# Transposes of x and of LayerNorm's output moved to the DMA queue, and P·V with V's two parts side by side

## The chip, the cores and the metric

The kernel runs on one core of a Trainium2 chip. The metric is device time in microseconds of one execution. Shorthand for the engines: PE is TensorE (PEld its weight loads), DVE VectorE, ACT ScalarE, POOL GpSimd, SP the engine whose queue issues nearly all DMAs.

## The reference, cut to what matters

Shapes: batch 4, 8 heads, sequence 576, head dimension 64, model dimension 512. All data are float32.

```
scores = (q @ k.T) / 8                      # per batch and head, 576 x 576
scores = where(scores >= max(scores) - tau, scores, -1e9)
attn   = softmax(scores)
x      = heads of (attn @ v) side by side   # 4 x 576 x 512
xn     = (x - mean(x)) / sqrt(var(x) + 1e-6) * g
x      = x + relu(xn @ w_ch1) @ w_ch2       # 512 -> 2048 -> 512
theta  = x @ w_theta
y      = w_tok_r @ (x * cos(theta)) + w_tok_i @ (x * sin(theta))   # over the tokens
u      = x + y
out    = u + relu(u @ w_ch)
```

## The kernel before

**Precision.** Most products are made in float16 with each factor split into a high part and a low part (the remainder), and three of the four partial products are added: high·high, high·low and low·high. The exceptions are the scores (float32) and all of batch 0's attention after the scores, which stays in float32 (the batches listed in `WHOLE`).

**Tiles.** Two batches form a pair `p`: 1152 tokens, nine tiles of 128. Tiles 0 to 3 belong to the even batch, 5 to 8 to the odd one, and tile 4, the tail, holds 64 tokens of each. Tiles are grouped by three for the LayerNorm and the MLP: group `(p, gi)`.

**Attention.** `couple(b, t, hp)` handles two heads of one tile of queries. Scores go to PSUM; DVE takes the row extreme, POOL adds tau, ACT masks and exponentiates into `ringE`; then the float16 high part and the low part are written to `ringP` (high 576 columns, low 512 and 64 columns beside them), and one DMA transpose from SP's queue turns 128x1152 of it into `PT`, nine blocks of 128x128. The product P·V (`pvmm`) takes for each of five key blocks the high P against V's high part (65 columns, the last being ones, so that the sum of the row comes with it) and against V's low part (64 columns), and then four low P blocks against V's high part: 14 products per head, 28 per couple. `evict` copies 128x130 from PSUM to `x`, on ACT or DVE. A tail couple has the two heads' tails in one tile, so its weights are 64 columns wide.

**LayerNorm and the MLP.** `ln_group` normalizes three tiles, transposes each with four float32 PE transposes (L1163) into PSUM, and evicts them as a high and a low part into `ringX`, which has two places. A copy goes to DRAM for later. `mlp1` (L701) and `mlp2` (L724) then run the first 12 of 16 column chunks of the MLP during the attention (`p_A`, `chA`); the last four chunks follow after the attention for all six groups (`p_B`, `c`).

**Theta, token mixing, channel product.** When a pair's x is final, a power-of-two scale is taken from the sum of its squares (L1457, L619 to L625). `transposes(b)` turns batch b's tiles with four float32 PE transposes each (L1525), and writes high and low parts, scaled, into `x1T`; the tail tile is turned once for both batches. `thetas` (L1573), `make_z` (cosine and sine, L1647 to L1660, and the parts of z, L296 and L309), `mix` (L1737) and `chan` (L1795) follow. The order in the code is: x, theta, z of batch 0; x, theta of batch 1; mix 0, z 1, channel 0, mix 1; x, theta, z of batch 2; channel 1; x, theta of batch 3; mix 2, z 3, channel 2, mix 3, channel 3. `x1T` has two places, so batch 2's waits for the end of channel 0.

**The order of the work.** Every step is an `op` with dependencies, slots of buffers that it acquires and releases, and a cost in nanoseconds for each engine that may run it. A planner (`Plan`) plays this through, gives each step to an engine, and writes the instructions out in that order; each engine's queue runs in order, DMAs of SP included. On PE the ready step with the lowest `key` goes first: attention has low keys, the first MLP part higher ones, so that MLP blocks fill what attention leaves. After the plan the chip keeps the order and only waits on semaphores.

Of the kernel before, what the change touches and what calls it, by code (L numbers as in the profile page):

```python
# [9 lines left out]
F16 = mybir.dt.float16  # L10
# [65 lines left out]
MT = 2  # L76
IDLE = 200.0
NTINY = 960
BUSY = 0.7
LATE = 25000.0  # L80
CX = [0, 760.0, 1250.0]
CHA, CHV, CHG = [0, 680.0, 1160.0], [0, 690.0, 1290.0], [0, 758.0, 1370.0]
CLV, CLG = [0, 930.0, 1600.0], [0, 1206.0, 2060.0]
# [187 lines left out]
def tile_kernel(  # L271
# [79 lines left out]
    rY = Res("y", 0)  # L351
    rXs = Res("x", NXS)
    rN = Res("xn", 2)
    rG = Res("g", 8)
    rR = Res("raw", NRAW)
    rQ, rK = Res("q", NQ), Res("k", NK)
# [102 lines left out]
    op(warmup, [k_ones], (warm,), (warm,), T=4000, key=-1e9)  # L459


    def cvt(src, shape, hi, lo, name, start=(), acq=(), kind="cvt", peak=None, late=None, early=False):


        n = 1
        for s_ in shape:
            n *= s_
        sl = Slot(rRe if early else rR)
        st = {}

        def s0(e):
            if early:
                raw = rawe[sl.i // 2][:, sl.i % 2]
            else:
                raw = (lp if sl.i < NRAW else later["wb"]).tile([128, 512, 2], I32, tag=str(sl), name=f"raw_{name}")
            rw = st["rw"] = raw[:, 0:n, :]
            if len(shape) == 2:
                dst = rw.rearrange("p (c k) two -> p c (k two)", c=shape[0])
            else:
                dst = rw.rearrange("p k two -> p (k two)")  # L480
            Q.dma_start(dst, src)

        sa = Slot(rN)

        def s1(e):
            st["a"] = lp.tile([128, 576], F32, tag=str(sa), name=f"a_{name}")[:, 0:n]
            if e is A:
# [37 lines left out]
        def s5(e):  # L525
            if late:
                V.scalar_tensor_tensor(out=lo(), in0=st["w"], scalar=late(), in1=hi(), op0=ALU.mult, op1=ALU.subtract)
            else:
                sub(e, lo(), st["w"], f(hi()))

        kw = dict(kind=kind)
        o = load = op(s0, start, tuple(acq) + (sl,), Q=1800, **kw)
        oa = op(s1, [o], [sa], A=ac(n), V=vc(n, .7), **kw)
        ob = op(s1b, [o], A=ac(n), **kw)
        if peak:
            o = op(s2a, [oa], V=vc(n, 1.1) + 80.0, **kw)
# [12 lines left out]

        return (load, end) if late else end([])  # L550
# [182 lines left out]
    class Keys:  # L733


        def __init__(self, b, hp, prev):
# [64 lines left out]
                                scalar1=0x7F800000, scalar2=None, op0=ALU.bitwise_and)  # L801

            def one(e):
                G.memset(st["va"][:, 0].rearrange("p t (j c) -> p t j c", j=2)[:, :, :, 64:65], 1.0)

            def hi16(e):
                A.activation(out=heads(0), in_=raw(), func=AF.Copy, scale=st["sc"])
# [20 lines left out]
            o = self.sc = op(s3, [o], V=150, **kd)  # L828
            o = op(hi16, [o], A=822, **kd)
            l = op(lo16, [o], (), (sv,), V=1130, G=2200, **kd)  # L830
            o1 = op(one, [o_n], G=130, **kd)
            self.vready = [op(other, [l, o1], A=300, V=230, **kd)]

    class Queries:
# [15 lines left out]
    def couple(b, t, hp):  # L850
# [38 lines left out]
        def pvmm(w, out, j, cs):  # L889
# [4 lines left out]
                             rhs=d.st["raw"][:, t, j * 65:j * 65 + 65], start=(t == 0), stop=(t == 4))  # L894
                return
            va, pt = d.st["va"], w["pt"]
            seq = []
            for t in range(4):
                seq.append((pt[:, t, cs], va[:, 0, t], 65))
                seq.append((pt[:, t, cs], va[:, 1, t], 64))  # L900
            seq.append((pt[:, 4, cs], va[:, 0, 4], 65))
            seq.append((pt[:, 4, cs], va[:, 1, 4], 64))
            for t in range(4):
                seq.append((pt[:, 5 + t, cs], va[:, 0, t], 65))
            for k, (l, r, n) in enumerate(seq):
                T.matmul(out[:, j * 65:j * 65 + n], lhsT=l, rhs=r[:, j * 65:j * 65 + n], start=(k == 0),  # L906
                         stop=(k == len(seq) - 1))

        def pv(e):
            if "o" not in cp:  # L910
# [8 lines left out]
        def evict(e):  # L919

            pr = slice(64 * odd, 64 * odd + 64) if last else slice(0, 128)
            if tile_ not in raw:
                raw[tile_] = xs.tile([128, 520], F32, tag=str(xrl), name=f"x_{p}_{t}")
            copy(e, raw[tile_][pr, hp * 130:hp * 130 + 130], cp["o"][pr, 0:130])

        o = op(pv, pts + d.vready + [first_pv.get(tile_)], (spv,) + sx_,
               [w["spt"] for w in us] + [d.sva] + ([cp["s16"]] if whole else []), T=(PVT if whole else 950), kind="att", **kw)
        first_pv.setdefault(tile_, o)
        done = x_ops.setdefault(tile_, [])
        done.append(op(evict, [o, d.sc] + done[:1], (), (spv,), V=290, A=275, kind="evict", **kw))  # L930
        if len(done) == (8 if last else 4):
            scaled(tile_)

# [168 lines left out]
    def ln_group(p, gi, base):  # L1102
# [44 lines left out]
        for t in range(nt):  # L1147
            sn, ms = Slot(rN), Slot(rM)

            def norm(e, t=t, sn=sn):  # L1150
# [5 lines left out]
                else:  # L1156
                    V.tensor_scalar(out=st["xn", t], in0=x[p, t0 + t], scalar1=rs[:, 0, t:t + 1],
                                    scalar2=rs[:, 1, t:t + 1], op0=ALU.mult, op1=ALU.add)

            def trans(e, t=t, ms=ms):  # L1160
                st["pt", t] = m_tile(ms, [128, KB, 128], f"ptr_{nm}_{t}")
                for c in range(KB):
                    T.transpose(st["pt", t][:, c, :], st["xn", t][:, c * 128:(c + 1) * 128], ident)  # L1163
# [5 lines left out]
            def lo(e, t=t):  # L1169
                cs = slice(t * 128, (t + 1) * 128)  # L1170
                sub(V, st["xt"][:, :, 1, cs], st["pt", t], st["xt"][:, :, 0, cs])

            o = first = op(norm, [o_rs, first] + last_tr, (sn,), A=808, V=vc(512, .95), kind="ln")
            o = op(trans, [o, k_pool] + trs[-1:], (ms,) if trs else (ms, sx), (sn,), T=460, key=key - 95.0)
# [323 lines left out]
    def transposes(b):  # L1498
# [5 lines left out]

        def alloc():
            if "t" not in st:
                y = later["yp"].tile([128, KB, 2, S], F16, tag=str(sl), name=f"x1T{b}")
                st["t"] = [y[:, :, a] for a in range(2)]
            return st["t"]

        for t in range(5):
            if t == 4 and odd:
                def tail2(e):
                    for a in range(2):
                        copy(e, alloc()[a][:, :, 512:576], tails[p]["t"][:, :, a, 64:128])
                st["ops"].append(op(tail2, [tails[p]["op"]] + st["ops"][:1], (), (tails[p]["sl"],),
                                    A=2 * ac(256), V=2 * vc(256, .95)))
                continue
            ms = Slot(rM)
            ss = {}  # L1520

# [12 lines left out]

            def dst(a, t=t):
                if t < 4:
                    return alloc()[a][:, :, t * 128:(t + 1) * 128]
                if "t" not in tails[p]:
                    i = tails[p]["sl"].i
                    tails[p]["t"] = hbuf[i // 2][:, i % 2].rearrange("p a (c k) -> p c a k", c=KB)  # L1540
# [12 lines left out]
            else:  # L1553
                tails[p]["op"] = o

                def tail1(e):
                    for a in range(2):
                        copy(e, alloc()[a][:, :, 512:576], tails[p]["t"][:, :, a, 0:64])
# [363 lines left out]
```

## Time and profile before

| | |
|---|---|
| median of 3 runs | 833.95 us (833.41 to 834.34) |
| the profiled execution | 833.26 us, of which the span is 831.5 us |
| PE busy | 821.0 us, 99% of the span |
| DVE, ACT, POOL busy | 621.0, 535.0, 355.8 us |
| granted clock of TensorE | 0.999 on average |
| DMA transposes | 108, all of P |

The profile is of one execution. A row of instructions in order of time has the start, the duration, the engine, the line, the operation, output and inputs, shape, and how many such instructions are merged in it; in brackets the idle time of the engine before it and what ended that. Rows that group instructions give the count, busy time and mean of one. Line numbers are those of the kernel before.

### The profile page before, as it was taken

To read this page: it belongs to the slowest core of one execution; us is meant where nothing else is said; L and a number is where in the kernel's file an instruction comes from. 1 tells how busy PE (TensorE), PEld (TensorE's weight loads), DVE (VectorE), ACT (ScalarE), POOL (GpSimd) and SP (SyncE) were. 2 spreads that over 40 slices of the span, in tenths; PEclk is the share of its full clock that TensorE was granted. 3 is DMA by queue.
4 is the path that set the end of the run, shared out by engine and by line. 5 is a ranking of instruction groups with operands and counts; after the bars stand their busy time and mean duration, and the time that the engine had idled before them with its cause. 6 is when DMAs were issued, how large, how long until landed. Compare 5 with 4: busy or idle time off the path is not lost. (4 is left out here: it accounts for less than half of the span.)

```text
span 831.5 us, 17300 instructions
## 1 busy us (share of the span) xinstructions
PE 821.0 (99%) x6625; PEld 543.4 (65%) x6625; DVE 621.0 (75%) x1279; ACT 535.0 (64%) x987; POOL 355.8 (43%) x444
## 2 busy tenths in 40 slices
PE   9999999999999999999999999999999999999997
PEld 8888866655566576666565555555555777667776
DVE  4878799999687887787557756766577693799943
ACT  5899999999588788888535543554476351564602
POOL 1332478787285465656321212221153250465611
PEclk9999999999999999999999999999999999999999
DMA  8433699894579799697563421744033010010011
GB/s 230 143 99 122 196 207 170 187 208 97 122 132 206 137 233 184 119 165 141 131 168 94 169 94 48 249 162 177 1 97 120 27 46 13 1 44 15 16 43 58
DMA packets 173235, 101.20 MB, mean 122 GB/s; under 512 B 136289, under 2 KB 154209, under 8 KB 173153
## 3 DMA queue, kind: packets, MB, share of 16 engines
q1 hardware_dynamic: 172864, 100.10, 49.5%
q8 instruction: 52, 0.85, 0.4%
q14 instruction: 31, 0.25, 0.1%
q10 hardware_dynamic: 288, 0.00, 0.0%
HBM read 52.50 MB, written 15.73 MB: 82 GB/s over the span
## 5 line engine op out<-in xcount | busy, mean ns | idle before, releaser
L701 PEld LDWEIGHTS <-w 128*128 128x128 f16 x1152 | 110.5, 98 | 80.7 <-issue 7.3
L701 PE MATMUL p_A<-ringX,w 128*128 128x384 f16 x864 | 149.9, 326 | 0.0
L724 PE MATMUL chA<-w,hbuf 128*128 128x512 f16 x648 | 149.2, 379 | 0.0
L724 PEld LDWEIGHTS <-hbuf 128*128 128x128 f16 x864 | 82.5, 99 | 93.6 <-issue 5.4
L979 DVE TENSOR_SCALAR_CACHE_REDUCE ringE<-S,ncoef 128x576 f32<-128x576 f32 x144 | 112.7, 812 | 27.2 <-PE S L878 21.1
L309 POOL TENSOR_TENSOR ringP<-ringE,ringP 128x512 f16<-128x512 f32 (+2 forms) x110 | 109.2, 1004 | 21.0 <-ACT ringP L296 16.1
L995 ACT ACTIVATE ringE<-ringE,tiny 128x576 f32<-128x576 f32 x144 | 105.5, 770 | 2.0 <-POOL tiny L987 1.0
L878 PE MATMUL S<-kf,qf 64*128 64x288 f32 (+1 forms) x576 | 98.5, 426 | 0.0
L1737 PE MATMUL y<-tok,z 128*128 128x288 f16 x768 | 97.2, 286 | 0.0
L1737 PEld LDWEIGHTS <-z 128*128 128x128 f16 x768 | 75.1, 98 | 19.2
L1021 ACT ACTIVATE ringE<-ringE,ntaup 128x576 f32<-128x576 f32 x108 | 78.6, 764 | 0.1
L707 ACT ACTIVATE hbuf<-p_A 128x384 f16<-128x384 f32 x72 | 35.2, 488 | 63.1 <-PE p_A L701 62.6
L878 PEld LDWEIGHTS S<-kf,qf 64*128 64x128 f32 (+1 forms) x576 | 56.9, 186 | 19.5 <-issue 4.5
L906 PEld LDWEIGHTS <-PT 128*128 128x128 f16 (+1 forms) x1680 | 57.3, 100 | 12.8 <-issue 5.4
L300 POOL TENSOR_SCALAR ringP<-ringE 128x576 f16<-128x576 f32 x63 | 44.7, 712 | 36.8 <-ACT ringE L1021 30.4
L906 PE MATMUL pv<-va,PT 128*128 128x65 f16 (+3 forms) x1680 | 60.2, 193 | 0.0
L1213 DVE SCALAR_TENSOR_TENSOR x<-chA,qs,x 128x512 f32<-128x512 f32 x54 | 40.3, 747 | 25.5 <-PE chA L724 25.3
L710 DVE SCALAR_TENSOR_TENSOR hbuf<-p_A,hbuf 128x384 f16<-128x384 f32 x72 | 39.6, 551 | 22.7 <-ACT hbuf L707 22.2
L724 PE MATMUL c<-w,hbuf 128*128 128x512 f16 x216 | 51.0, 379 | 0.0
L701 PE MATMUL p_B<-ringX,w 128*128 128x384 f16 x288 | 50.7, 326 | 0.0
L1795 PE MATMUL o<-x1T,cw 128*128 128x288 f16 x384 | 48.0, 286 | 1.3 <-DVE x1T L1770 1.3
L309 DVE TENSOR_TENSOR ringP<-ringE,ringP 128x512 f16<-128x512 f32 (+2 forms) x58 | 44.0, 768 | 2.9 <-ACT ringP L296 1.4
(228 smaller groups left out, 1392.8 us busy)
## 6 DMA issues: line engine op xcount, KB each, us to landing
raw_w<-in_w SPq DMA_DIRECT2D x20, 512.0 KB, 4.5
rawe<-in_w SPq DMA_DIRECT2D x12, 512.0 KB, 4.8
raw_tok<-in_wtok SPq DMA_DIRECT2D x12, 432.0 KB, 4.4
qf<-in_qT SPq DMA_DIRECT2D x20, 256.0 KB, 3.5
kf<-in_kT SPq DMA_DIRECT2D x16, 288.0 KB, 4.0
xscr<-x SPq DMA_DIRECT2D x18, 256.0 KB, 2.4
xl<-xscr SPq DMA_DIRECT2D x18, 256.0 KB, 5.1
out<-uo SPq DMA_DIRECT2D x16, 288.0 KB, 2.1
```

The costliest lines, as they stand in the source:

```text
L300: G.tensor_scalar(out=out, in0=in_, scalar1=1.0, scalar2=0.0, op0=ALU.mult, op1=ALU.add)
L309: e.tensor_tensor(out=out, in0=a, in1=b, op=ALU.subtract)
L701: T.matmul(st["ps"][:, :n], lhsT=ch.w1(a, c), rhs=xt()[:, c, bb, :n], start=(kk == 0), stop=(kk == 11))
L724: T.matmul(ps, lhsT=h[:, a, t * 128:(t + 1) * 128], rhs=ch.w2(bb), start=(first and (a, bb) == M2[0]), stop=(stop and (a, bb) == M2[2]))
L878: T.matmul(w["S"][:, n, 0:288], lhsT=qd.q["f"][r, hp], rhs=d.k["f"][r, n * 288:(n + 1) * 288], start=True, stop=True)
L906: T.matmul(out[:, j * 65:j * 65 + n], lhsT=l, rhs=r[:, j * 65:j * 65 + n], start=(k == 0), stop=(k == len(seq) - 1))
L979: V.tensor_scalar(out=st["e"].rearrange("p (a k) -> p a k", a=2), in0=st["S"][:, :, 0:288], scalar1=ncoef, scalar2=None, op0=ALU.mult, op1 ...
L995: A.activation(out=st["e"], in_=st["e"], func=AF.Prelu, bias=cp["thr"][:, j:j + 1], scale=-1.0, alpha=STEEP)
L1021: A.activation(out=e_of(ws), in_=e_of(ws), func=AF.Exp, bias=ntaup, scale=1.0)
L1213: V.scalar_tensor_tensor(out=x[p, t0 + t], in0=st["ch", t], scalar=chunks[i].quad.inv, in1=x[p, t0 + t], op0=ALU.mult, op1=ALU.add)
L1737: T.matmul(st["ps"][n][:, 0:288], lhsT=a, rhs=w[:, n * 288:(n + 1) * 288], start=(k == 0 and q == 0), stop=(k == 8 and q == 2))
L1795: T.matmul(st["ps"][n][:, 0:288], lhsT=w[:, cs], rhs=d["t"][a][:, kk, n * 288:(n + 1) * 288], start=(kk == 0 and q == 0), stop=(kk == 3 an ...
```

## The change

- `XQ = (0, 1, 2)`: for batches 0, 1 and 2 `transposes(b)` writes the scaled high and low part of each x tile, in its own orientation, into a buffer of float16 (one of the slots for raw weights), high and low blocks of 128 columns in turn, and one DMA transpose of 128x1024 on SP's queue turns it into `x1T`. Batch 3 goes by PE as before.
- `LNQ = ((1, 0), (1, 1))`: for these two groups `ln_group` does the same with the normalized tiles, into `ringX`.
- `PVW = (2, 3)`: for these two batches V's low part gets a 65th column of zeros, and P's high block is multiplied with V's high and low part in one product of 130 columns; the low P blocks go into the high part's columns. The two parts are added when they leave PSUM: `evict` becomes a reduction over two on DVE.

```diff
+NX16 = 2
+LNQ = ((1, 0), (1, 1))
+PVW = (2, 3)
+XQ = (0, 1, 2)
...
+    rX16 = Res("x16", NX16)
...
             def one(e):
-                G.memset(st["va"][:, 0].rearrange("p t (j c) -> p t j c", j=2)[:, :, :, 64:65], 1.0)
+                for a in range(2 if b in PVW else 1):
+                    G.memset(st["va"][:, a].rearrange("p t (j c) -> p t j c", j=2)[:, :, :, 64:65], 1.0 - a)
...
+            for t in range(9):
+                n = 130 if t < 5 else 65
+                T.matmul(out[:, j * 130:j * 130 + n], lhsT=pt[:, t, cs], rhs=va[:, :, t, js] if t < 5 else va[:, 0, t - 5, js],
+                         start=(t == 0), stop=(t == 8))
...
-            copy(e, raw[tile_][pr, hp * 130:hp * 130 + 130], cp["o"][pr, 0:130])
+            to = raw[tile_][pr, hp * 130:hp * 130 + 130]
+            if whole or b not in PVW:
+                copy(e, to, cp["o"][pr, 0:130])
+            else:
+                o2 = cp["o"][pr, 0:260].rearrange("p (j a c) -> p j a c", j=2, a=2)
+                V.tensor_reduce(out=to.rearrange("p (j c) -> p j c", j=2), in_=o2.rearrange("p j a c -> p j c a"), op=ALU.add,
+                                axis=mybir.AxisListType.X)
...
+            if (p, gi) in LNQ:
+                o = first = op(norm, [o_rs, first], (sn,), A=808, V=vc(512, .95), kind="ln")
+                o = op(hi_t, [o], (s16,), A=ac(512), V=vc(512, .95), G=CHG[1] - 60.0, kind="lnev")
+                o = op(lo_t, [o], (), (sn,), V=vc(512, V2), G=gc(512), kind="lnev")
+                o = op(turn_t, [o] + xt[:1], () if xt else (sx,), (s16,), Q=1800, kind="lnev")
+                xt.append(o)
+                continue
...
+            def hi_t(e, parts=parts, xin=xin):
+                scopy(e, parts()[:, :, 0, :], xin(), px(p, X_S))
+            def lo_t(e, parts=parts, xin=xin):
+                V.scalar_tensor_tensor(out=parts()[:, :, 1, :], in0=xin(), scalar=px(p, X_S), in1=parts()[:, :, 0, :], op0=ALU.mult,
+                                       op1=ALU.subtract)
+            def turn_t(e, parts=parts, turned_=turned_):
+                Q.dma_start_transpose(out=turned_(), in_=parts().rearrange("p c a k -> p (c a k)"))
...
+            if b in XQ:
...
+                o = op(hi_t, [xf[p, t0 + t], sx_ops[p], st.get("hi")], acq, A=ac(512), V=vc(512, .95), G=CHG[1] - 60.0, kind="ev")
+                st["hi"] = o
+                o = op(lo_t, [o], (), (x_slot[p, t0 + t],), V=vc(512, V2), kind="ev")
+                o = op(turn_t, [o] + st["ops"][:1], (), (s16,), Q=1800, kind="ev")
```

## Rows read from the trace of the kernel before

**Rows 1.** Page, part 1: busy us (share of the span) and instructions.

```profile
PE 821.0 (99%) x6625; PEld 543.4 (65%) x6625; DVE 621.0 (75%) x1279; ACT 535.0 (64%) x987; POOL 355.8 (43%) x444
```

**Rows 2.** Busy time by stretch: length, engines, clock, DMA share, GB/s.

```profile
232.00:300.00 68.00, 68.00 (x694) 43.18 (x691) 56.94 (x124) 56.41 (x98) 41.78 (x58) 1.00 0.88 170
300.00:340.00 40.00, 40.00 (x407) 25.89 (x406) 29.10 (x71) 33.81 (x63) 22.34 (x37) 1.00 0.95 181
...
683.00:708.00 25.00, 25.00 (x206) 20.07 (x205) 9.56 (x17) 2.33 (x3) 0.00 (x0) 1.00 0.12 48
708.00:760.00 52.00, 50.36 (x330) 32.31 (x329) 44.91 (x62) 31.28 (x51) 29.95 (x27) 1.00 0.06 24
```

**Rows 3.** Waits of PE: us in total, times, longest.

```profile
PE pt L1525 <- DVE r_t L1591: 1.6, 1, 1.6
```

**Rows 4.** Groups of PE by line and shape: count, busy, mean.

```profile
L1163 PE MATMUL ptr<-ident,xn 128*128 128x128 f32 x72 | 10.8, 278 | 0.0
...
L1525 PE MATMUL pt<-ident,xl 128*128 128x128 f32 x72 | 9.4, 274 | 1.6 <-DVE r_t L1591 1.6
```

**Rows 5.** PE in order of time, transposes of batch 2's x.

```profile
707.58 1.91 PE L1525 MATMUL pt<-ident,xl 128*128 128x128 f32 x16
709.32 1.63 PE L1795 MATMUL o<-x1T,cw 128*128 128x288 f16 x12
```

**Rows 6.** Line 1042, P's DMA transposes: ns min/median/max; us to landing.

```profile
L1042 SPq DMA_TRANSPOSE PT<-ringP x108: 1242/1337/2912, 99.6 to 422.7; - x108
...
DMA to landing us min/median/max: 3.2/3.6/6.7
```

**Rows 7.** DVE in order of time, the last step of x's scale.

```profile
589.44 0.15 DVE L625 TENSOR_SCALAR cs<-cs 128x1 int32<-128x1 int32 x1 [0.66 <-POOL cs L622]
```

**Rows 8.** PE in order of time, batch 0's theta and first mixing's tail.

```profile
594.51 10.52 PE L1573 MATMUL th<-th,x1T 128*128 128x512 f16 x48
...
648.78 0.90 PE L1737 MATMUL y<-tok,hbuf 128*128 128x288 f16 x6
```

**Rows 9.** SP's queue in order of time, P's transposes.

```profile
309.02 8.56 SPq L1042 DMA_TRANSPOSE PT<-ringP  x4
...
381.28 24.54 SPq L1042 DMA_TRANSPOSE PT<-ringP  x10
```

**Rows 10.** PE in order of time, LN's transposes and P·V around 310.

```profile
303.97 0.60 PE L1163 MATMUL ptr<-ident,xn 128*128 128x128 f32 x4
304.40 1.01 PE L906 MATMUL pv<-va,PT 128*128 128x65 f16 x28
305.25 0.63 PE L1163 MATMUL ptr<-ident,xn 128*128 128x128 f32 x4
...
306.69 0.60 PE L1163 MATMUL ptr<-ident,xn 128*128 128x128 f32 x4
...
312.27 1.07 PE L906 MATMUL pv<-va,PT 128*64 128x65 f16 x28
313.28 1.47 PE L724 MATMUL chA<-w,hbuf 128*128 128x512 f16 x6
...
323.39 1.14 PE L701 MATMUL p_A<-ringX,w 128*128 128x384 f16 x6
```

**Rows 11.** Groups of DVE by line and shape: the copy of P·V.

```profile
L298 DVE COPY x<-pv 128x130 f32<-128x130 f32 x18 | 5.2, 286 | 4.3 <-PE pv L906 2.7 <-PE pv L893 1.3
```

**Rows 12.** POOL in order of time, last part of z's tail.

```profile
639.49 1.15 POOL L309 TENSOR_TENSOR hbuf<-r_t,hbuf 128x512 f16<-128x512 f32 x1 [1.02 <-ACT hbuf L296]
```

**Rows 13.** DVE in order of time, last part of group (1,2).

```profile
447.43 0.68 DVE L309 TENSOR_TENSOR ringX<-ptr,ringX 128x512 f16<-128x512 f32 x1
```

**Rows 14.** PE in order of time, the end of attention.

```profile
420.30 2.69 PE L906 MATMUL pv<-va,PT 128*128 128x65 f16 x84
...
455.29 5.04 PE L701 MATMUL p_A<-ringX,w 128*128 128x384 f16 x30
```

More of the change, by code (lines that the diff above doesn't have):

```diff
@@ L459, in tile_kernel, with raw_tile @@
     op(warmup, [k_ones], (warm,), (warm,), T=4000, key=-1e9)
+    def raw_tile(slot, name):
+        return (lp if slot.i < NRAW else later["wb"]).tile([128, 512, 2], I32, tag=str(slot), name=name)
     def cvt(src, shape, hi, lo, name, start=(), acq=(), kind="cvt", peak=None, late=None, early=False):
@@ L474, in s0 @@
             else:
-                raw = (lp if sl.i < NRAW else later["wb"]).tile([128, 512, 2], I32, tag=str(sl), name=f"raw_{name}")
+                raw = raw_tile(sl, f"raw_{name}")
             rw = st["rw"] = raw[:, 0:n, :]
@@ L830, in __init__ @@
             l = op(lo16, [o], (), (sv,), V=1130, G=2200, **kd)
-            o1 = op(one, [o_n], G=130, **kd)
+            o1 = op(one, [o_n], G=260 if b in PVW else 130, **kd)
             self.vready = [op(other, [l, o1], A=300, V=230, **kd)]
@@ L896, in pvmm @@
             va, pt = d.st["va"], w["pt"]
[L897 to L907, printed above, removed]
+            js = slice(j * 65, j * 65 + 65)
+            if b not in PVW:
+                seq = [(t, va[:, a, t], 65 - a) for t in range(5) for a in range(2)] + [(5 + t, va[:, 0, t], 65) for t in range(4)]
+                for k, (t, r, n) in enumerate(seq):
+                    T.matmul(out[:, j * 65:j * 65 + n], lhsT=pt[:, t, cs], rhs=r[:, j * 65:j * 65 + n], start=(k == 0),
+                             stop=(k == len(seq) - 1))
+                return
+            for t in range(9):
+                n = 130 if t < 5 else 65
+                T.matmul(out[:, j * 130:j * 130 + n], lhsT=pt[:, t, cs], rhs=va[:, :, t, js] if t < 5 else va[:, 0, t - 5, js],
+                         start=(t == 0), stop=(t == 8))
         def pv(e):
@@ L923, in evict @@
                 raw[tile_] = xs.tile([128, 520], F32, tag=str(xrl), name=f"x_{p}_{t}")
-            copy(e, raw[tile_][pr, hp * 130:hp * 130 + 130], cp["o"][pr, 0:130])
+            to = raw[tile_][pr, hp * 130:hp * 130 + 130]
[5 more added lines that the diff above has]
+                                axis=mybir.AxisListType.X)
         o = op(pv, pts + d.vready + [first_pv.get(tile_)], (spv,) + sx_,
-               [w["spt"] for w in us] + [d.sva] + ([cp["s16"]] if whole else []), T=(PVT if whole else 950), kind="att", **kw)
+               [w["spt"] for w in us] + [d.sva] + ([cp["s16"]] if whole else []), T=(PVT if whole else 850 if b in PVW else 950), kind="att", **kw)
         first_pv.setdefault(tile_, o)
         done = x_ops.setdefault(tile_, [])
-        done.append(op(evict, [o, d.sc] + done[:1], (), (spv,), V=290, A=275, kind="evict", **kw))
+        done.append(op(evict, [o, d.sc] + done[:1], (), (spv,), kind="evict", **(dict(V=290, A=275) if whole or b not in PVW else dict(V=430)), **kw))
         if len(done) == (8 if last else 4):
@@ L1158, in norm, with parts, hi_t, lo_t @@
                                     scalar2=rs[:, 1, t:t + 1], op0=ALU.mult, op1=ALU.add)
+            s16 = Slot(rX16)
+            def parts(t=t, s16=s16):
+                if ("x16", t) not in st:
+                    st["x16", t] = ap.tile([128, KB, 2, 128], F16, tag=str(s16), name=f"xn16_{nm}_{t}")
+                return st["x16", t]
+            def hi_t(e, t=t, parts=parts):
+                copy(e, parts()[:, :, 0, :], st["xn", t].rearrange("p (c k) -> p c k", c=KB))
+            def lo_t(e, t=t, parts=parts):
+                sub(e, parts()[:, :, 1, :], st["xn", t].rearrange("p (c k) -> p c k", c=KB), parts()[:, :, 0, :])
+            def turn_t(e, t=t, parts=parts):
+                st["xt"] = ringX[:, sx.i]
+                Q.dma_start_transpose(out=st["xt"][:, :, :, t * 128:(t + 1) * 128].rearrange("p c a k -> p (c a) k"),
+                                      in_=parts().rearrange("p c a k -> p (c a k)"))
             def trans(e, t=t, ms=ms):
@@ L1506, in alloc @@
             if "t" not in st:
-                y = later["yp"].tile([128, KB, 2, S], F16, tag=str(sl), name=f"x1T{b}")
-                st["t"] = [y[:, :, a] for a in range(2)]
-            return st["t"]
+                st["y"] = later["yp"].tile([128, KB, 2, S], F16, tag=str(sl), name=f"x1T{b}")
+                st["t"] = [st["y"][:, :, a] for a in range(2)]
+            return st["y"]
         for t in range(5):
@@ L1514, in tail2, with parts @@
                     for a in range(2):
-                        copy(e, alloc()[a][:, :, 512:576], tails[p]["t"][:, :, a, 64:128])
+                        copy(e, alloc()[:, :, a, 512:576], tails[p]["t"][:, :, a, 64:128])
                 st["ops"].append(op(tail2, [tails[p]["op"]] + st["ops"][:1], (), (tails[p]["sl"],),
                                     A=2 * ac(256), V=2 * vc(256, .95)))
+                continue
+            s16 = Slot(rR)
+            ss = {}
+            def parts(ss=ss, s16=s16, t=t):
+                if "t" not in ss:
+                    ss["t"] = raw_tile(s16, f"x16_{b}_{t}").bitcast(F16).rearrange("p k two -> p (k two)")[:, 0:1024].rearrange(
+                            "p (c a k) -> p c a k", c=KB, a=2)
+                return ss["t"]
@@ new lines, in xin, with turned_ @@
+            def xin(t=t):
+                return x[p, t0 + t].rearrange("p (c k) -> p c k", c=KB)
+            def hi_t(e, parts=parts, xin=xin):
[3 more added lines that the diff above has]
+                                       op1=ALU.subtract)
+            def turned_(t=t):
+                if t < 4:
+                    return alloc()[:, :, :, t * 128:(t + 1) * 128].rearrange("p c a k -> p (c a) k")
+                i = tails[p]["sl"].i
+                tails[p]["t"] = hbuf[i // 2][:, i % 2].rearrange("p a n -> p (a n)").rearrange("p (c a k) -> p c a k", c=KB, a=2)
+                return tails[p]["t"].rearrange("p c a k -> p (c a) k")
@@ new lines, in turn_t, with tail1 @@
+            def turn_t(e, parts=parts, turned_=turned_):
+                Q.dma_start_transpose(out=turned_(), in_=parts().rearrange("p c a k -> p (c a k)"))
+            if b in XQ:
+                acq = [s16]
+                if t == 0:
+                    acq.append(sl)
+                if t == 4:
+                    tails[p] = {"sl": Slot(rG, 3)}
+                    acq.append(tails[p]["sl"])
+                o = op(hi_t, [xf[p, t0 + t], sx_ops[p], st.get("hi")], acq, A=ac(512), V=vc(512, .95), G=CHG[1] - 60.0, kind="ev")
+                st["hi"] = o
+                o = op(lo_t, [o], (), (x_slot[p, t0 + t],), V=vc(512, V2), kind="ev")
+                o = op(turn_t, [o] + st["ops"][:1], (), (s16,), Q=1800, kind="ev")
+                if t < 4:
+                    st["ops"].append(o)
+                else:
+                    tails[p]["op"] = o
+                    def tail1(e):
+                        for a in range(2):
+                            copy(e, alloc()[:, :, a, 512:576], tails[p]["t"][:, :, a, 0:64])
+                    st["ops"].append(op(tail1, [o] + st["ops"][:1], (), (tails[p]["sl"],), A=2 * ac(256), V=2 * vc(256, .95)))
@@ L1536, in dst @@
                 if t < 4:
-                    return alloc()[a][:, :, t * 128:(t + 1) * 128]
+                    return alloc()[:, :, a, t * 128:(t + 1) * 128]
                 if "t" not in tails[p]:
@@ L1557, in tail1 @@
                     for a in range(2):
-                        copy(e, alloc()[a][:, :, 512:576], tails[p]["t"][:, :, a, 0:64])
+                        copy(e, alloc()[:, :, a, 512:576], tails[p]["t"][:, :, a, 0:64])
                 st["ops"].append(op(tail1, [o] + st["ops"][:1], (), (tails[p]["sl"],), A=2 * ac(256), V=2 * vc(256, .95)))
```

## The prediction

> **What bounds the kernel now.** I read the page's busy times first, then busy time by stretch, then what TensorE waited for, and last its instructions in order of time around each edit. TensorE (PE) is busy 821.0 of 831.5 us, the next engine, VectorE (DVE), 621.0 [rows 1]. That a pipelined PE looks busy proves little, so the stretches count: from 232 to 340 us (attention of batches 2 and 3 mixed with the first MLP) and from 683 to 708 (token mixing of batch 1) PE has no gap at all, at a granted clock of 1.00, its 2.4 GHz level, while DVE sits at 73 to 84% in the attention and at 9.56 of 25 us in the mixing [rows 2]. Only from 708 to 760 does PE lose 1.64 us, nearly all of it in one wait of 1.6 us of an x transpose for DVE [rows 2, 3]. So PE's own instruction stream sets the end, and an edit is worth the PE time from its first instruction to the start of what follows. The rows' busy column is no price: a burst's last matmul overlaps the next burst. I take start to start.
>
> **The transposes of x.** Batch 0 has five tiles, batch 1 four (its tail is shared) and batch 2 five: 14 tiles of four float32 transposes, 56 of the 72 of that line [rows 4]. Sixteen of them, the largest of batch 2's bursts, run from 707.58 to 709.32, where the next matmul starts: 0.109 us each [rows 5]. 56 x 0.109 = 6.1 us leave PE.
>
> What comes instead: per tile a scaled float16 copy, a subtraction (both were there already, reading PSUM; now they read SBUF) and one DMA transpose of 128x1024 on SP's queue. The trace has 108 DMA transposes of 128x1152: 1.34 us of queue each, landing after 3.2 to 6.7, median 3.6 us [rows 6]. Is the longer way hidden?
>
> Batch 2: its copies need the buffer that batch 0's channel product frees, which stands ahead of batch 1's mixing in the order of the code; its theta product comes only after that mixing, at 708. From 683 to 708 DVE, ScalarE and POOL are nearly idle and DMA stands at 0.12 [rows 2]; five tiles of about 1.4 us of copies and 2.1 us of transfer fit into 25 us. It also takes the copies out of the crowded stretch 708:760 (DVE 44.91 of 52 us). Batch 1: its x is final before batch 0's theta products, and blocks of the second MLP part follow those, likewise hidden. Batch 0 is the delicate one. The scale of x is ready at 589.6 [rows 7]; copy and subtraction take about 1.4 us, a transpose 3.6 us to land, so the first tile is there at about 594.6, where the first theta matmul stood at 594.51 [rows 8]. Four transposes in a row occupy SP for 8.56 us, 2.1 us each, in a crowded stretch [rows 9]; a theta tile is 12 products of 512 columns, 12 x 0.213 = 2.6 us at 2.4 GHz, so the later tiles arrive faster than PE consumes them, and until then PE has blocks of the MLP's second part. Cost: 0 to 0.5 us, taken as 0. If that cover were gone, each us of late landing would be a us.
>
> The Trainium skill, DMA: Bandwidth & Descriptors, section "Latency and other measured facts", says that a DMA transpose with a non-contiguous middle dimension runs at 261 GB/s against 350 to 400 contiguous, a hit of some 30%. That speaks against this edit, because the new destinations are strided rows of x's buffer where P's were whole. By it a turn in a crowd would take 2.1 x 1.3 x 8/9, an estimate of 2.4 us, still under a theta tile, and the sum would stay.
>
> **LN's two groups.** Groups (1,0) and (1,1), three tiles each: 24 of the 72 transposes of that line [rows 4]. One tile takes 0.43 us (303.97 to 304.40) [rows 10]: 6 x 0.43 = 2.6 us off PE. Six DMA transposes are added where DMA is busy 0.88 to 0.95 [rows 2]. The last tile of (1,0) is turned at 306.69, its group's first product starts at 323.39, 16 us later [rows 10]; so a landing of even 6.7 us is covered, and the P transposes that queue behind a turn are 2 us late each time, while PE runs MLP blocks. Cost taken: 0; without the cover it is those 2 us for each of six turns.
>
> **PV in one product.** A full couple of heads issues 28 products of 64 or 65 columns; it will issue 10 of 130 and 8 of 65 (columns: 1810 before, 1820 after). 28 take 0.85 us (304.40 to 305.25) [rows 10], 30.4 ns each, of which 65 columns at 2.4 GHz are 27.1 and 3.3 are fixed. A product of 130 has no row: with the same fixed part 57.5 ns; at best bare columns, 54.2; at worst twice a 65, 60.8. New couple: 10 x 57.5 + 8 x 30.4 = 818 against 851 ns. I take the 0.033, the ends being 0 and 0.066, because the fixed part is the nearest row's own. 32 couples: 1.0 us (0 to 2.1). The 8 tail couples load weights of 64 columns and are slower, 1.01 us for 28 (312.27 to 313.28) [rows 10], 36.1 ns each. If the load sets that, a product of 130 hides it, and 10 x 57.5 + 8 x 36.1 saves 0.146 us; if it is a fixed part of 9 ns an instruction, 0.09; at worst nothing. I take 0.12, so 1.0 us (0 to 1.2). Together 2.0 us (0 to 3.3).
>
> On those tail couples, the Trainium skill, TensorEngine Tiling (Array Packing), section "Restrictions", says that column tiling disables fast weight load. The trace agrees so far as the 64-column bursts are the slower ones; by the rule the saving there is the upper figure, 1.2 us, and the sum 10.9.
>
> Against it stands the eviction: a copy of 128x130 from PSUM, on ScalarE or DVE, becomes a DVE reduction over 260 elements, 40 times. DVE's copy took 0.286 us [rows 11]; the reduction lies between that and twice it, 0.57; I take 0.45, nearer the upper end, because it reads twice the elements. DVE gains 40 x 0.45 = 18 us less the copies it loses (half of the 18, 3 us), 15 us over some 200; in the attention of rows 2 its 86 of 108 us (80%) would be about 87%: beside PE as long as PE has MLP blocks to run. If that cover went, 40 x 0.17 = 7 us would come out.
>
> **The sum.** 6.1 + 2.6 + 2.0 = 10.7 us. The profiled execution took 833.26 us, 1.76 around its span, which stay; it lies 0.69 under the median. 833.26 - 10.7 = 822.6, at the level of the median **823.3**. The 1.64 us of gaps in 708:760 I leave where they are.
>
> **Rivals.** (1) The attention edits buy nothing, because DMA and the elementwise engines, not PE, pace that stretch, and PE only runs MLP blocks earlier and idles later. For it: DMA at 0.95, and 15 more us on DVE. Against it: no gap in PE from 232 to 340. It would keep the x part alone, 833.95 - 6.1 = about 828.
>
> (2) Theta and z of batch 0 become the wait. The last of z's parts for the first mixing is written at 640.6 [rows 12] and read at 648.78 [rows 8], 8.1 us later. Batches 0 and 1 take 36 x 0.109 = 3.9 us of PE out of the path between, so 4.2 us of slack are left. Should the landings be at the slowest of rows 6 (issue 2.9, landing 6.7), the fifth theta tile would start some 7 us late, 3 us would be lost, and twice that if the second batch suffers as well: 826 to 829.
>
> (3) Slower: the matmuls that cover the end of attention run out. Group (1,2), the last, needs the last attention tile. Its parts are done at 448.1 [rows 13]; its first product starts at 455.29, when (1,1)'s matmuls are through [rows 14]: 7.2 us of slack. The attention had another 14 us between a long row of P transposes, issued by 405.8 [rows 9], and the PV behind it at 420.30 [rows 14]. Should each of the six turns hold up the queue by 5 us, between the median landing and the slowest, 30 us, and the reductions add 7, the 37 us would overrun the 21 us of slack by 16 and more than eat the sum: 833.95 - 10.7 + 16 = 839; at a delay of 34 us it is 836. It decides from 21 us of delay on, and from 32 us the kernel is slower than before. Against it: transfers overlap, a queue slot is 2 us and not 5.
>
> (4) The whole order is planned anew, so waits of 1 to 3 us can open anywhere, or the present ones close. With the gap at 740 gone and PV at its upper end: 833.95 - 6.1 - 2.8 - 3.3 - 1.6 = 820; with 6 us of new waits 829.
>
> (5) It cancels out, within 0.2%, where (1) and (2) come together with such waits.
>
> **How the numbers follow.** Forecast with the good half of (4), 817 to 827: 0.66. (1) 0.10; (2) with the bad half of (4) 0.09; (5) 0.05; (3) 0.10. The forecast's own range is 819 to 827; the range for 8 times in 10 runs from 817 to 831. Faster by over 0.2% (under 832.3; about what can be told from no change): 0.85; within: 0.05; slower: 0.10.
>
> **What would show it.** Right: 16 PE transposes left of the x line and 48 of LN's; 128 DMA transposes; 1280 PV products, a couple in about 0.82 us; PE still without gaps from 232 to 440 and around 590 to 610; theta of batch 2 directly behind the mixing of batch 1; PE's busy time near 810. Wrong: PE waiting at the first theta matmul for a DMA, at the first product of (1,2) for LN, or at PV for the reduction; a product of 130 columns at 61 ns; a granted clock below 1.00 in a stretch before the last. A gap of over 10 us in PE anywhere would overturn the forecast.

## The result, and the profile after

The changed kernel takes **821.38 us** (median of 4 runs, 820.92 to 822.14); the kernel before took 833.68 (4 runs, 833.28 to 834.34). The ratio is 0.9853, with a 95% interval of 0.9836 to 0.9870: 12.3 us faster. The forecast was 823.3 us, or 10.7 us off the profiled execution. The profiled execution after took 821.73 us with a span of 819.9, so 11.6 us less span than before.

First the page of the changed kernel, the row that answers to [rows 1]: busy us (share of the span) and instructions.

```profile
PE 811.4 (99%) x6145; PEld 533.8 (65%) x6145; DVE 622.7 (76%) x1291; ACT 531.7 (65%) x966; POOL 371.2 (45%) x462
```

PE has 480 instructions less: 56 + 24 transposes, and 40 couples with 10 products fewer each. Its busy time fell by 9.6 us, to the forecast "near 810", and the span by 2 us more than that. So besides PE work, idle time of PE is gone. DVE's busy time rose by 1.7 us only and POOL's by 15.4 (against [rows 1]). The waits show which (engine, line, tile, what it waited for: us in total, times, longest). After:

```profile
PE pvs L798 <- ACT va L791: 1.0, 1, 1.0
PE warm L454 <- POOL ones L420: 1.0, 1, 1.0
PE pw_w L607 <- ACT tiny L601: 1.0, 1, 1.0
PE pt L1617 <- DVE r_t L1683: 0.2, 1, 0.2
```

Before, the same list had one more row beside that of [rows 3]:

```profile
PE o L1795 <- DVE x1T L1770: 1.3, 1, 1.3
```

The first three waits after are as before. Of the 1.6 us of [rows 3] 0.2 is left, and the 1.3 us at batch 2's channel product is gone.

Busy time by stretch after (length, PE, PEld, DVE, ACT, POOL, clock, DMA share, GB/s); the first three rows answer to the last three of [rows 2], shifted by the time saved ahead of them:

```profile
292.00:332.00 40.00, 40.00 (x345) 27.03 (x344) 33.04 (x77) 32.63 (x58) 29.18 (x43) 1.00 0.95 186
...
674.00:700.70 26.70, 26.70 (x220) 21.32 (x219) 16.33 (x25) 6.35 (x11) 3.81 (x3) 1.00 0.46 95
700.70:752.00 51.30, 51.08 (x337) 32.87 (x336) 43.09 (x59) 30.83 (x51) 27.93 (x26) 1.00 0.06 24
700.00:790.00 90.00, 89.78 (x653) 63.80 (x651) 71.07 (x94) 47.92 (x80) 45.61 (x39) 1.00 0.07 27
```

In the attention PE still has no gap. In the mixing of batch 1 (second row) DVE does 16.33 us where it did 9.56, and DMA stands at 0.46 instead of 0.12: that is batch 2's x, turned under the mixing. Behind it PE idles for 0.22 us of 90. In the kernel before, the 90 us from 700 on read so:

```profile
700.00:790.00 90.00, 87.04 (x629) 61.57 (x627) 75.40 (x97) 49.53 (x82) 48.58 (x40) 1.00 0.05 17
```

That is 2.96 us idle. Now PE in order of time after (start, duration, engine, line, operation, tiles, shape, count), for [rows 5, 8, 10]:

```profile
0.98 7.31 PE L454 MATMUL warm<-ones 128*128 128x128 f32 x40 [0.98 <-POOL ones L420]
...
305.87 0.98 PE L915 MATMUL pv<-va,PT 128*128 128x130 f16 x18
306.68 0.81 PE L732 MATMUL chA<-w,hbuf 128*128 128x512 f16 x3
...
316.53 1.01 PE L915 MATMUL pv<-va,PT 128*64 128x130 f16 x18
317.48 1.24 PE L887 MATMUL S<-kf,qf 64*128 64x288 f32 x8
...
583.60 2.06 PE L1498 MATMUL px<-cs,ones 128*128 128x1 f32 x18
...
595.26 2.75 PE L1665 MATMUL th<-th,x1T 128*128 128x512 f16 x12
597.85 2.10 PE L732 MATMUL c<-w,hbuf 128*128 128x512 f16 x9
599.79 7.93 PE L1665 MATMUL th<-th,x1T 128*128 128x512 f16 x36
...
636.05 4.21 PE L1829 MATMUL y<-tok,z 128*128 128x288 f16 x33
...
700.73 10.52 PE L1665 MATMUL th<-th,x1T 128*128 128x512 f16 x48
...
713.68 11.92 PE L1887 MATMUL o<-x1T,cw 128*128 128x288 f16 x96
725.44 2.37 PE L1829 MATMUL y<-tok,z 128*128 128x288 f16 x18
...
802.67 11.93 PE L1887 MATMUL o<-x1T,cw 128*128 128x288 f16 x96
```

And the same milestones in the kernel before:

```profile
0.97 6.16 PE L449 MATMUL warm<-ones 128*128 128x128 f32 x40 [0.97 <-POOL ones L415]
...
586.51 2.06 PE L1457 MATMUL px<-cs,ones 128*128 128x1 f32 x18
...
642.90 2.37 PE L1737 MATMUL y<-tok,z 128*128 128x288 f16 x18
...
711.23 10.52 PE L1573 MATMUL th<-th,x1T 128*128 128x512 f16 x48
...
734.47 1.63 PE L1737 MATMUL y<-tok,z 128*128 128x288 f16 x12
...
814.98 11.92 PE L1795 MATMUL o<-x1T,cw 128*128 128x288 f16 x96
```

This gives the account. Up to the sum for x's scale (`px`) the lead is 2.9 us; the 40 matmuls that warm TensorE up at the start, which the change doesn't touch, took 1.15 us longer in this profile, so the attention is worth 4.1. At the first mixing it is 6.85: another 3.95, which is 36 transposes of 0.109 us. At the mixing of batch 2 it is 9.03: another 2.2, the 20 transposes of batch 2. At the last channel product it is 12.3 (814.98 against 802.67): another 3.3, of which 2.7 is idle time of PE that is gone, all of it behind 725. 4.1 + 3.95 + 2.2 + 3.3 is 13.5; less the 1.15 at the start that is the 12.3. From that product's start to the end of the span this profile takes 17.2 us and the one before 16.5, a difference of 0.7 that no edit explains; so 11.6 of the 12.3 are left in the span. The medians, which no single start or end decides, differ by 12.3.

The new DMA transposes on SP's queue after, x's (L1587, the two into `hbuf` are the tail tiles) and LN's (L1190) beside P's (L1057); count, ns min/median/max, first and last start, then us from issue to landing:

```profile
L1587 SPq DMA_TRANSPOSE x1T<-x x12: 1231/1288/2145, 589.7 to 685.5; - x12
L1587 SPq DMA_TRANSPOSE hbuf<-x x2: 1232/1272/1311, 597.4 to 686.9; - x2
...
DMA to landing us min/median/max: 3.0/3.3/5.0
...
L1190 SPq DMA_TRANSPOSE ringX<-xn x6: 1232/1351/1631, 316.3 to 397.0; - x6
...
DMA to landing us min/median/max: 3.3/4.1/5.1
...
L1057 SPq DMA_TRANSPOSE PT<-ringP x108: 1242/1345/3082, 100.8 to 419.9; - x108
...
DMA to landing us min/median/max: 3.2/3.7/7.2
```

With the 108 of P that makes the 128 that the prediction named. x's turns land a little sooner than P's, and LN's six, in the busiest stretch, a little later. P's own are about where [rows 6] had them. Five of x's in a row on the queue:

```profile
589.67 7.44 SPq L1587 DMA_TRANSPOSE x1T<-x  x5
```

### The profile page after: what moved, and what is told of

Read it like the earlier page. It is cut to its first block, busy times and chain, and to the rows that moved or that the text cites. A ratio compares the mean times of both kernels' runs of the same rounds, so it can differ in the third digit from the quotient of the medians.

```text
span 819.9 us, 16404 instructions
## 1 busy us (share of the span) xinstructions
PE 811.4 (99%) x6145; PEld 533.8 (65%) x6145; DVE 622.7 (76%) x1291; ACT 531.7 (65%) x966; POOL 371.2 (45%) x462
## 4 chain that ended last, share of the span: by engine, by line
PE 95%; ACT 2%; DVE 1%; issue 1%; POOL 0%; DVEq 0%; ACTq 0%; POOLq 0%
PE chA L732 17%; PE p_A L709 17%; PE y L1829 13%; PE S L887 11%; PE p_B L709 6%; PE c L732 6%; PE th L1665 5%; PE pv L902 5%; PE o L1887 4%; PE pv L915 4%; PE tm L965 2%; PE pv L910 2%; PE warm L454 1%; PE th_t L1665 1%; PE ptr L1196 1%
## 5 line engine op out<-in xcount | busy, mean ns | idle before, releaser
L304 POOL TENSOR_SCALAR ringP<-ringE 128x576 f16<-128x576 f32 x59 | 42.6, 725 | 37.0 <-ACT ringE L1036 34.3
L1887 PEld LDWEIGHTS <-cw 128*128 128x128 f16 x384 | 37.6, 98 | 9.7
L308 ACT ACTIVATE x1T<-u,cs 128x576 f16<-128x576 f32 x16 | 12.3, 770 | 47.7 <-DVE u L1856 41.9
```

The costliest lines, as they stand in the source:

```text
L304: G.tensor_scalar(out=out, in0=in_, scalar1=1.0, scalar2=0.0, op0=ALU.mult, op1=ALU.add)
L1887: T.matmul(st["ps"][n][:, 0:288], lhsT=w[:, cs], rhs=d["t"][a][:, kk, n * 288:(n + 1) * 288], start=(kk == 0 and q == 0), stop=(kk == 3 an ...
```

## The experiments

In the expectations A is the account that I held when the run was sent (each edit is worth the PE time that it removes; from the two traces, the closed gaps come from batch 2's x), and B is the rival named there. Differences are against the median of the kernel before on the same chip; where the changed kernel itself is the measure, its ratio 0.9853 is compared.

**x alone.** LN and P·V as before.

```diff
-LNQ = ((1, 0), (1, 1))
-PVW = (2, 3)
+LNQ = ()
+PVW = ()
```

> Only the x transposes of batches 0 to 2 go by DMA; LN's stay on PE and P.V is as before. Theory A (each edit is worth the PE time it takes away, and batch 2's x also closes the gaps of PE between 708 and 790 us): 56 x 0.109 = 6.1 us plus about 2.9 us of gaps, 833.7 - 9.0 = 824.7 us, PE without a gap over 0.5 us after 700. Theory B (the closed gaps come from LN's and P.V's edits, or from the new order as a whole): 833.7 - 6.1 = 827.6 us, with the wait of about 1.6 us for DVE at batch 3's transposes still there.

825.84 against 833.67 us, ratio 0.9903 (0.9888 to 0.9918): 7.8 us off, between the two. PE behind 700 is as full as in the changed kernel (89.77 of 90 us), so the closed gaps belong to x. About 1 us of what is missing is lost in the attention, where no edit acts, only the new order: x's scale (`px`) starts at 588.47 against 586.51, of which 0.95 us is a longer warm-up at the start. PE has these waits that neither kernel had:

```profile
PE pv L910 <- DVE tiny L589: 0.9, 1, 0.9
PE pv L910 <- ACT x L300: 0.5, 1, 0.5
```

In return the wait of 1.0 us for `va` is down to 0.3. From 0 to 240 us PE is busy 236.5 us, 237.1 before; so only 0.6 of the 1 us is idle time.

**P·V alone, LN alone, and batch 2's x alone.**

```diff
 # P.V alone
+LNQ = ()
+XQ = ()
 # LN alone
+PVW = ()
+XQ = ()
 # batch 2's x alone
+LNQ = ()
+PVW = ()
+XQ = (2,)
```

> Only the product of 130 columns for batches 2 and 3, with the reduction at eviction; all transposes on PE. Theory A (PE sets the end of the attention stretch): 32 couples x 0.031 + 8 tail couples x 0.06 = 1.5 us off, 832.2 us. Theory B (the attention stretch is paced by DVE and DMA, to which the reductions add 14 us): no gain or a loss, 833.7 us or more.

832.92 us, ratio 0.9988 (0.9979 to 0.9997): 0.75 us off, with an interval of 0.25 to 1.75 us. The gain is there and small; A's 1.5 lies inside, "nothing" doesn't. In the trace `px` starts at 585.43 against 586.51, behind a warm-up longer by 0.26 us: 1.3 us.

> Only LN of groups (1,0) and (1,1) turned by DMA. Theory A (PE sets the end): 24 x 0.109 = 2.6 us off, 831.1 us. Theory B (DMA, busy 0.9 in this stretch, paces it, and six more turns take the place of what PE saves): 833.7 us or more, with waits of PE at P.V or at the first MLP product.

831.13 us, ratio 0.9971 (0.9960 to 0.9982): 2.5 us off (1.5 to 3.3), as 6 x 0.43 says. In this kernel and in the one with P·V alone the waits of 1.6 and 1.3 us stand unchanged.

> Only the x of batch 2 goes by DMA. Theory A (its 20 transposes leave PE, and its copies leave the crowded stretch behind 708 us, which closes the gaps of PE there): 2.2 + 2.9 = 5.1 us off, 828.6 us. Theory B (the gaps close for another reason): 2.2 us off, 831.5 us, with the wait of about 1.6 us for DVE still there.

828.31 us, ratio 0.9935 (0.9922 to 0.9947): 5.4 us off. The 20 transposes are worth 2.2; here, without any other edit, the wait of 1.6 us is down to 0.2 and that of 1.3 is gone. Of the edits, batch 2's x is the one that closes the gaps.

**The transposes of batches 0 and 1 alone.**

```diff
+LNQ = ()
+PVW = ()
+XQ = (0, 1)
```

> Only the x of batches 0 and 1 goes by DMA. Theory A (PE's own time counts and the landings are hidden): 36 x 0.109 = 3.9 us off, 829.8 us, the two waits of PE behind 708 us still there (about 2.9 us). Theory B (batch 0's theta waits for its landings, or z is late for the first mixing): less than 2 us off, 831.7 us or more, with a wait of PE at theta or at the mixing.

830.89 against 833.92 us, ratio 0.9969 (0.9958 to 0.9981): 3.0 us off where the PE time says 3.9. PE waits nowhere at theta or the first mixing; the waits of 1.6 and 1.3 us are as in the kernel before, and before 240 us the new order has opened ones of 0.9, 0.5 and 0.2 us and closed the one of 1.0 for `va` (PE busy 236.4 us from 0 to 240, 237.1 before).

**Do the gaps close by the order alone, with no PE time saved?** The kernel before, with batch 2's transposes still on PE, but put by their key to the head of batch 1's mixing.

```diff
-        key = nkey() if b else KEY0
+        key = (nkey() - (1.5 if b == 2 else 0.0)) if b else KEY0
```

> The kernel before with one edit: PE's transposes of batch 2's x, and so their copies, stand ahead of batch 1's token mixing instead of behind it. PE has exactly the work of before. Theory A (the gaps behind 708 us close because batch 2's x is ready when the mixing ends, so theta starts earlier and the elementwise work behind it too): about 2.7 us off without any PE time saved, 831.0 us. Theory B (they close only because transposes leave PE): no change, 833.7 us, with the waits of 1.6 and 1.3 us still there.

831.81 us, ratio 0.9976 (0.9966 to 0.9986): 2.1 us off (1.2 to 2.8) without a single PE instruction less. Of PE's waits the two old ones are gone but for 0.2 us, and one of 0.9 is new (line numbers of the kernel before):

```profile
PE pt L1525 <- DVE x1T L1547: 0.9, 1, 0.9
PE pt L1525 <- DVE r_t L1591: 0.2, 1, 0.2
```

And in order of time its stretch behind the mixing:

```profile
710.89 0.90 PE L1737 MATMUL y<-tok,hbuf 128*128 128x288 f16 x6
711.62 10.52 PE L1573 MATMUL th<-th,x1T 128*128 128x512 f16 x48
...
724.58 11.92 PE L1795 MATMUL o<-x1T,cw 128*128 128x288 f16 x96
```

Theta follows the mixing at once and all 96 products of channel 1 stand behind it, as in the changed kernel. In the kernel before twelve of the 96 had to cover the copies of x [rows 5], and 84 were left for the longer wait; that this is why PE waited is argued, not shown. The price is the 0.9 us where the early transposes wait for their own evictions. This run moves the copies of x out of the stretch as well: DVE is busy 70.32 of the 90 us from 700 on, 75.40 before. So it shows that the place of batch 2's transposes and copies closes the gaps, and not which of the two does it, theta's early start or the lighter DVE.

**Is it the work taken off DVE?** The changed kernel with five dead DVE operations, as long as the subtractions (0.69 us each), that theta has to wait for; four of the five run behind batch 1's mixing, the first under it.

```diff
+                if b == 2:
+                    def late(e, t=t):
+                        ...
+                        V.scalar_tensor_tensor(out=later["dead"], in0=later["dead"], scalar=1.0, in1=later["dead"], op0=ALU.mult,
+                                               op1=ALU.subtract)
+                    o = op(late, [o, ylast[0]], V=690, kind="ev")
```

> The changed kernel with five idle DVE operations of about 0.75 us each (one per tile of batch 2, on a buffer of their own, result unused) placed behind batch 1's token mixing and ahead of batch 2's theta, where the subtractions of batch 2's x stood in the kernel before; nothing else is added, and PE's work is that of the changed kernel. Theory A (the gaps of PE between 708 and 790 us closed because DVE work left that stretch): most of the 2.9 us of gaps come back, 823 to 824.5 us. Theory B (they closed because of the order of PE's own instructions there, transposes ahead of theta): nothing comes back, 821.4 to 822 us.

822.06 against 834.29 us, ratio 0.9858 (0.9841 to 0.9874): as the changed kernel. One wait of 1.2 us opens (PE's mixing for POOL's `z`; PE busy 88.75 of the 90 us from 700 on), but the two old ones don't come back. DVE's busy time there is 73.29 us, so half of the 4.3 us that had gone is back; and 12 channel products stand ahead of theta again, with 30 more inside it. The old waits stay away all the same. So this run bears out neither account alone, that of the lighter DVE or that of the twelve products.

**More of the same: batch 3's x, LN's five groups, three groups, P·V of three batches.**

```diff
 # batch 3 as well
+XQ = (0, 1, 2, 3)
 # LN, five groups
+LNQ = ((0, 0), (0, 1), (0, 2), (1, 0), (1, 1))
 # LN, three groups
+LNQ = ((0, 2), (1, 0), (1, 1))
 # P.V, three batches
+PVW = (1, 2, 3)
```

> Batch 3's x goes by DMA as well, the other edits as in the changed kernel. Theory A (PE's own time counts): 16 x 0.109 = 1.7 us off, 819.7 us. Theory B (its buffer comes free only when batch 1's channel product ends, so copies of 1.4 us and a landing of 3.3 us stand ahead of its first theta product, in the stretch where DVE is at 84%): the gaps come back, 821.4 us or more.

825.07 us, ratio 0.9889 (0.9874 to 0.9903): 3.0 us slower than the changed kernel. PE in order of time at batch 3's theta:

```profile
734.16 12.15 PE L1665 MATMUL th<-th,x1T 128*128 128x512 f16 x48 [3.86 <-DMA x1T<-x]
746.14 1.63 PE L1829 MATMUL y<-tok,z 128*128 128x288 f16 x12
```

Here PE has no work ready to cover the turns: batch 3's landings are waited for, 3.9 us, and the 48 products then take 12.15 us instead of 10.52. The granted clock is 0.90 from 730 to 735, 0.75 from 735 to 740 and 1.00 from 740 on:

```profile
730.00:735.00 5.00, 1.14 (x6) 0.30 (x4) 5.00 (x7) 3.54 (x7) 2.77 (x2) 0.90 0.85 210
735.00:745.00 10.00, 10.00 (x42) 4.32 (x41) 8.08 (x12) 4.09 (x6) 6.13 (x5) 0.88 0.41 91
```

> LN by DMA in five groups, the three of the first pair added. Theory A (PE's own time counts wherever PE has no gap): nine tiles x 0.435 = 3.9 us off, 817.5 us. Theory B (from 100 to 200 us DMA is busy 0.85 to 1.07 and DVE 98%, so nine more turns there make P's transposes late and PE waits): 821.4 us or more, with waits of PE at P.V or at the MLP's first product before 240 us.

827.50 us, ratio 0.9917 (0.9903 to 0.9932): 5.3 us slower than the changed kernel, where nine tiles less on PE promised 3.9 us of gain. Busy time in steps of 5 us:

```profile
160.00:165.00 5.00, 2.47 (x34) 1.83 (x34) 5.00 (x9) 5.00 (x10) 5.00 (x6) 0.81 0.49 111
165.00:170.00 5.00, 4.19 (x31) 3.08 (x32) 5.00 (x9) 4.51 (x8) 4.12 (x4) 0.50 0.73 141
170.00:175.00 5.00, 5.00 (x40) 3.22 (x37) 5.00 (x13) 3.31 (x7) 3.96 (x6) 0.66 1.33 177
175.00:180.00 5.00, 4.97 (x51) 2.95 (x47) 4.68 (x13) 4.16 (x8) 3.70 (x6) 1.00 1.10 217
```

Around 160 us nothing but attention is ready for PE, and DVE (5.00 of 5), ACT and POOL set the pace; PE loses 3.3 us in three waits and then runs at the 1.2 GHz level (0.50) for a while. Here the cover that the prediction counted on, MLP blocks, isn't there: from 157 to 178 us PE has only attention and matmuls that fill time (`warm`).

> The changed kernel with LN of group (0,2) by DMA too, near 245 us, where DVE is below 90%. Theory A (a group outside the stretch where DVE is saturated gives back its PE time): 12 x 0.109 = 1.3 us off, 820.1 us. Theory B (its first product stands about 10 us behind its transposes, and a copy from SBUF plus a landing of 4 us under load use that up): 821.4 us or more, with a wait of PE before 260 us.

823.44 against 833.92 us, ratio 0.9876 (0.9863 to 0.9890): A's further gain fails here too, with some 2 us more than the changed kernel, though the two intervals overlap at their ends. Between 254 and 261 us PE has no MLP block, and the plan fills with 17 `warm` matmuls, 2 us together:

```profile
257.01 1.16 PE L462 MATMUL warm<-one 128*128 128x256 bf16 x9
...
260.12 1.05 PE L462 MATMUL warm<-one 128*128 128x256 bf16 x8
```

That is not the whole of it: a wait of 0.7 us for V's parts (`va`) opens at 254.5, and before 240 us PE has the waits of the run with x alone again (0.8 and 0.5 us, 0.5 us less busy from 0 to 240), at a place that this group doesn't touch.

> The product of 130 columns in batch 1 as well. Theory A (PE's own time counts): 16 couples x 0.031 + 4 x 0.06 = 0.7 us off, 820.7 us. Theory B (20 reductions of 0.42 us more on DVE, which is at 98% from 120 to 200 us, have no cover): about 20 x 0.42 = 8 us more on DVE less the copies it did, part of it on the path: 823 to 828 us.

822.61 us, ratio 0.9866 (0.9851 to 0.9881): with 0.8 us of PE time on offer (16 couples of 0.033 and 4 tails of 0.06 us) it is not faster than the changed kernel, and if anything 1 us slower, which the intervals don't decide. PE has new waits of 0.9, 0.7 and 0.3 us and loses an old one of 1.0; from 100 to 590 us it is busy 1.0 us less than in the changed kernel, more than the edit had to give.

**Does the reduction cost anything?** The eviction copies the high part alone and leaves V's low part out.

```diff
-                V.tensor_reduce(out=to.rearrange("p (j c) -> p j c", j=2), in_=o2.rearrange("p j a c -> p j c a"), op=ALU.add,
-                                axis=mybir.AxisListType.X)
+                copy(e, to.rearrange("p (j c) -> p j c", j=2), o2[:, :, 0, :])
```

> The changed kernel with the eviction of batches 2 and 3 a copy of the high part's columns alone, on ACT or DVE as before; the low part of V is left out of the result. It takes 40 reductions of 0.42 us from DVE. Theory A (they lie beside PE): 821.4 us within 0.5. Theory B (DVE paces part of the attention of the second pair): 817 to 820 us.

822.51 us, ratio 0.9865 (0.9851 to 0.9878): no gain over the changed kernel with 40 reductions gone. B's 820 us or less is out; A's 821.4 within 0.5 is missed by 0.6 us, which the interval covers. They lie beside PE.

None of the versions beats the changed kernel.

## Why the prediction was right, and where its sizes were off

**The bound.** PE's instruction stream sets the end: its busy time fell by 9.6 us and the time by 12.3. The lead grew at the milestones as start-to-start times of PE had it: up to the mixing of batch 2, by 10.2 us of the 10.7 forecast. The rest of the measured 12.3 comes from a term that the sum had at nothing.

**x's transposes: 6.1 us, right.** 3.95 + 2.2 in the trace. Batch 0's landings, the delicate place, are covered: theta begins at 595.26, 11.7 us behind `px`, and PE fills the 11.7 us with `px` and MLP blocks without a gap. The way there was longer than forecast: from the end of the scale (586.67) to the first turn's issue (589.67) 3.0 us, not 1.4. The turns themselves follow each other faster: five in a row take 7.44 us, 1.5 us each, where the prediction had 2.1. The Trainium skill, DMA: Bandwidth & Descriptors, section "Latency and other measured facts", would have made a turn into strided rows some 30% slower; the trace doesn't show it (at least 3.0 us to land against P's 3.2, in the median 3.3 against 3.7), and the measurement decides, so far as times to landing can tell. LN's turns, into strided rows as well, have medians of 3.2 to 4.1 us over the runs, P's 3.4 to 3.7.

**LN: 2.6 us, right** (2.5 alone). The turns land after at most 5.1 us, and PE has no gap in that stretch.

**P·V: 2.0 us forecast, 1.5 found in the trace, 0.75 measured alone (0.25 to 1.75).** The full couple takes 0.81 us (305.87 to 306.68), and 0.81 to 0.83 wherever an MLP block follows it, the forecast 0.818: the price with the same fixed part for a product of 130 columns as for one of 65 came out. The mis-sized term is the tail couple: 0.95 us (316.53 to 317.48) where 0.89 was forecast, against 1.01 before, so 0.06 saved and not 0.12, 0.5 us for the eight and not 1.0. That is below both readings that the prediction weighed, the load that sets the pace (0.146) and a fixed part of 9 ns (0.09). The Trainium skill, TensorEngine Tiling (Array Packing), section "Restrictions", states that column tiling disables fast weight load; the trace doesn't bear out the saving of 1.2 us that followed from it. The reduction was forecast at 0.45 us and takes 0.42:

```profile
L938 DVE TENSOR_REDUCE x<-pv 128x130 f32<-128x260 f32 x32 | 13.5, 424 | 6.4 <-PE pv L915 6.3
```

**The gaps: "I leave where they are" was the step that failed.** They closed, 2.7 us of idle time and 3.3 us of lead, more than all of the P·V edit, and the prediction had them only as part of rival (4). It counted 1.64 us, since its stretch ended at 760; the one of 1.3 us at batch 2's channel product lay behind that. And it said itself that theta of batch 2 would stand directly behind the mixing, without asking what the twelve channel products that had covered x's copies would cover next. That batch 2's x being turned before the mixing ends closes the gaps is shown by the run that only moves the transposes (2.1 us with no PE work removed), and that no other edit does it by the runs with each alone. How much of it is due to the emptier DVE (71.07 instead of 75.40 of 90 us), and how much to theta's early start and the twelve products, stays open: the run with dead DVE work had a wait of 1.2 us, but put back half of DVE's work only, and its order on PE had changed as well.

**DVE's load, beside the path.** The prediction had 15 us more on DVE in the attention. From 240 to 440 us it is 154.43 us instead of 148.35, 6 us more, and POOL 119.29 instead of 107.60: the new plan gave POOL more of the work. That cost PE nothing, and the run without the reductions gained nothing.

**The rivals.** (1) fell: LN alone brings its full size, P·V alone a gain clear of nothing. (2) fell: with batches 0 and 1 alone PE waits neither at theta nor at mixing. (3) didn't come; its mechanism, cover that runs out, came in the run with five LN groups, not at the end of attention but at 160 us. (4) is real in both directions: the closed gaps, and the microsecond lost before x's scale in the runs with x alone, at a place that no edit touches. (Its 820 us has LN at 2.8 us, where LN's own section has 2.6; that moves it by 0.2.) Alone the three edits bring 7.8 + 2.5 + 0.75 = 11.1 us, together 12.3; that microsecond is about as large as the difference, which the intervals of the runs cover too.

## What to carry to other kernels

Where PE has no gap, moving a PE transpose to a DMA queue is worth its start-to-start time, as long as the stretch has independent PE work for the copies and the 3 to 5 us of the landing; look for that work at every place by itself, since the same edit taken one batch or three groups further cost 3 to 5 us. When a step leaves the critical engine, ask what had been covering it and what that work covers now. In a kernel whose order is planned anew, allow for a microsecond or so of waits opened or closed at places that the edit doesn't touch.

## What the runs showed of the hardware that was not expected

- A gap of PE can cost more than its length. In the run with five LN groups three waits, 3.3 us together between 161 and 169 us, went with granted clocks of 0.81, 0.50 and 0.66 in the 15 us from 160 on. In the run with batch 3's x a wait of 3.9 us was followed by 0.90 and 0.75 in the 10 us from 730 on, and by 48 products that took 1.6 us longer. The waits of 1.6 and 1.3 us in the kernel before left the clock at 1.00.
- The 40 warm-up matmuls at the start, the same in both kernels, took 6.16 us in one profile and 7.31 in the other, and 6.14 to 7.64 over the profiles of all runs here. In the first, PE starts 5 to 7 instructions a microsecond up to 4 us and 11 to 12 from then on; in the second 5 to 7 up to 6 us. The granted clock reads 1.00 all through in both. One profiled execution isn't exact to a microsecond.
